# The second MLP product by Strassen's seven block products, in blocks of 256 positions

## The chip, the cores and the metric

The kernel runs on one core of one Trainium2 chip. The metric is device time in microseconds (us). The engines are PE (TensorE: matmuls, and PEld, its weight loads), DVE (VectorE), ACT (ScalarE), POOL (GpSimd) and SP (SyncE, which issues most DMAs here).

## The reference

A block of a network on 2048 positions (S) with 512 features (D): a spectral filter by a two-dimensional Fourier transform, then an MLP with 1376 hidden features (F), each with layer normalization, modulated shift and scale, and a gate. All numbers are float32.

```python
mod = (_silu(c) @ w_mod).reshape(c.shape[0], 6, 1, -1)
sa, ca, ga, sb, cb, gb = (mod[:, 0], mod[:, 1], mod[:, 2], mod[:, 3], mod[:, 4], mod[:, 5])
h = _layernorm(x, axis=-1) * (1 + ca) + sa
x = x + ga * irfft2(rfft2(h) * (A_w_r + 1j * A_w_i))
h = _layernorm(x, axis=-1) * (1 + cb) + sb
u = h @ B_w1 + B_b1
x = x + gb * ((u * tanh(softplus(u))) @ B_w2)
```

## The kernel before

Three stages compute the spectral part, all on tiles of 128 positions. The first (`p1_*`) transforms rows and columns, the second (`p2_*`) multiplies by the filter, the third (`p3_col`, `p3_row`) transforms back and adds the result to `x`, which stays on the chip as 16 tiles of 128 positions by 512 features. The MLP follows.

Matmuls of the MLP take their operands as pairs of two F32R numbers, a high part and a low part (the rest of the subtraction), and a product is three matmuls: high by high, high by low, low by high. So each operand has to be split: ACT or DVE copies the high part, DVE or POOL subtracts it for the low part. The weights `w1` (`w1h`, `w1l`), the gated weights `w2`, the normalized input `h2` and the activations (`ah`, `al`) are all split like this.

The MLP before works on 4 blocks of 512 positions and, within a block, on 11 feature tiles (10 of 128 features and one of 96). `up(g)` makes one feature tile for 512 positions: 12 matmuls (three terms by four input tiles of 128). `mish(g)` applies Mish on ACT and splits the result. `down(g)` adds the tile's product with `w2` to four PSUM banks, one for each 128 positions: 12 matmuls of 512 columns. `down` runs two steps behind `up` (`LAG = 2`). After the last feature tile DVE adds the four banks to `x` and SP stores them. The normalized input of the next block is made meanwhile by `norm_pair` (ACT), `transpose_in` (PE) and `split_in` (ACT and DVE).

The order on each engine is written out by hand: under `tc.manual_schedule()` every engine runs its instructions in program order. Tiles of the pool `work` with one tag share two buffers (`buf(tag)`); a new tile waits until all users of the one before the last are done. The loop over `s` from 0 to 16 interleaves the third stage with the preparation of the MLP: at step `s` PE does `p3_col(s)`, whose result ACT copies to `e`, and then `p3_row(s - 1)`, which reads the copy; then DVE adds it to `x`. In the same loop SP loads `w1` in 12 pieces (`load_w1`, buffers of the tags `y` and `g2` in turn), ACT and POOL split them (`split_w1`), and from step 12 on `w2` is loaded, multiplied by the gate `gbr` on POOL (`load_w2`) and split by ACT and DVE (`split_w2`). `norm_sums` and `norm_scale` make the statistics for the second normalization. The loop after it runs `mlp(s)`.

Of the kernel before, what the change touches and what calls it, by code (L numbers as in the profile page):

```python
# [7 lines left out]
F32 = mybir.dt.float32  # L8
F32R = mybir.dt.float32r
# [10 lines left out]
LAG = 2  # L20
LEAD = 8
OUT = ("BBCC", "DDBB", "CCDD")
SPARE = "DCB"
# [3 lines left out]
def tile_spectral_block(ctx: ExitStack, tc: tile.TileContext, x_d, w1_d, b1_d, w2_d,  # L27
# [542 lines left out]
    act = ctx.enter_context(tc.tile_pool(name="act", bufs=LAG + 1))  # L570
    w1h = pm.tile([P, 4, F], F32R, name="w1h")
    w1l = pm.tile([P, 4, F], F32R, name="w1l")
    w1v = w1_d.rearrange("(k p) f -> p k f", p=P)
# [19 lines left out]
    def h2_tiles(b):  # L593
        if b % 2 == 0:
            h2[b] = [pm.tile([P, 4, 512], F32R, name=f"h2{i}", tag=f"h2{i}") for i in range(2)]
        else:
            h2[b] = [big.tile([P, 4, 512], F32R, name=f"h2{i}", tag=t) for i, t in enumerate(("cr", "ci"))]
# [4 lines left out]
    def transpose_in(n, tag):  # L602
        b, j = divmod(n, 4)
        if j == 0:
            h2_tiles(b)
        pts = [bank(tag), bank(tag)]
        for i, h in enumerate(st.pop(("h2", n))):
            for k in range(4):
                nc.tensor.transpose(pts[k // 2][:, (2 * (k % 2) + i) * P:(2 * (k % 2) + i + 1) * P],  # L609
                                    h[:, k * P:(k + 1) * P], ident)  # L610
        st["pt2", n] = pts

    def split_in(n):
        b, j = divmod(n, 4)
        pts = st.pop(("pt2", n))
        for g in range(2):
            t = buf("t")
            for e in range(2):
                k = 2 * g + e
                nc.scalar.activation(t[:, 256 * e:256 * e + 256], pts[g][:, 256 * e:256 * e + 256],  # L620
                                     AF.Identity, bias=cols[:, 1, 0, k:k + 1], scale=cols[:, 1, 1, k:k + 1])
            tv = t.rearrange("p (k s) -> p k s", k=2)
            hh, hl = (v[:, 2 * g:2 * g + 2, j * P:j * P + 256] for v in h2[b])
            nc.vector.tensor_copy(hh, tv)
            nc.vector.tensor_tensor(hl, tv, plain(hh), op=ALU.subtract)
# [22 lines left out]
    w2 = {}  # L648

    def load_w2(f):  # L650
        if f in (0, 6):
            w2[f // 6] = big.tile([P, 6, 2, D], F32R, name="w2", tag=("da", "db")[f // 6])
        rows = min(P, F - f * P)
        r = buf("y")[:rows]
        nc.sync.dma_start(r, w2_d[f * P:f * P + rows, :])
        nc.gpsimd.tensor_tensor(r, r, gbr[:rows], op=ALU.mult)  # L656
        st["w2", f] = r

    def split_w2(f):
        r = st.pop(("w2", f))  # L660
        w = w2[f // 6][:r.shape[0], f % 6]
        nc.scalar.copy(w[:, 0, :], r)
        nc.vector.tensor_tensor(w[:, 1, :], r, plain(w[:, 0, :]), op=ALU.subtract)
# [6 lines left out]
    ups, acts, out_ps = {}, {}, {}  # L670

    def up(g):
        b, f = divmod(g, NF)
        rows = min(P, F - f * P)
        ps = bank("C" if g < 2 else "A")[:rows]
        fs = slice(f * P, f * P + rows)
        hh, hl = h2[b]
        parts = [(w, h, k) for w, h in ((w1h, hh), (w1l, hh), (w1h, hl)) for k in range(4)]
        for i, (w, h, k) in enumerate(parts):
            nc.tensor.matmul(ps, w[:, k, fs], h[:, k, :], start=(i == 0), stop=(i == 11))  # L680
        ups[g] = rows, ps

    def mish(g):
        rows, ps = ups.pop(g)
        w = act.tile([P, 512], F32, name="mw", bufs=2)[:rows]
        ah = act.tile([P, 512], F32R, name="ah")[:rows]
        al = act.tile([P, 512], F32R, name="al")[:rows]
        nc.scalar.activation(w, ps, AF.Mish, bias=b1n[:rows, g % NF:g % NF + 1])  # L688
        nc.vector.tensor_copy(ah, w)  # L689
        nc.vector.tensor_tensor(al, w, plain(ah), op=ALU.subtract)  # L690
        acts[g] = ah, al

    def down(g):
        b, f = divmod(g, NF)
        ah, al = acts.pop(g)
        rows = ah.shape[0]
        if f == 0:
            out_ps[b] = [bank(t) for t in OUT[b % 3]]
        for j in range(4):
            for i, (a, w) in enumerate(((ah, 0), (ah, 1), (al, 0))):  # L700
                nc.tensor.matmul(out_ps[b][j], a[:, j * P:(j + 1) * P], w2[f // 6][:rows, f % 6, w, :],  # L701
                                 start=(f == 0 and i == 0), stop=(f == NF - 1 and i == 2))
        if f == NF - 1:
            for j in range(4):
                n = 4 * b + j
                nc.vector.tensor_tensor(x[:, n, :], x[:, n, :], out_ps[b][j], op=ALU.add)
                nc.sync.dma_start(ov[:, n:n + 1, :], x[:, n:n + 1, :])

    total = 4 * NF
    ctx.enter_context(tc.manual_schedule())  # L710

    def mlp(s):
        b, f = divmod(s, NF)
        nxt = 4 * (b + 1)
        if b < 3 and f in (3, 6):
            norm_pair(nxt + 2 * (f // 6))
        if b < 3 and f in (4, 7):
            transpose_in(nxt + 2 * (f // 7), SPARE[b])
        if 2 <= s < total:
            up(s)  # L720
            mish(s)
        if s >= LAG:
            down(s - LAG)
        if 2 <= s < 9:
            split_w2(s + 2)
        if 2 <= s < 8:
            load_w2(s + 3)
        if b < 3 and f in (4, 7):
            split_in(nxt + 2 * (f // 7))

    apply_gate()
    for s in range(N2 + 1):
        if s < N2:
            p3_col(s)
        if s < 12:
            load_w1(s)
        else:
            load_w2(s - 12)
        if s >= 1:
            p3_row(s - 1)  # L740
        if s in (7, 9):
            transpose_in(s - 7, "D")
        if 2 <= s < 14:
            split_w1(s - 2)
        if s >= 13:
            split_w2(s - 13)
# [12 lines left out]
    for g in range(2):  # L759
        mish(g)  # L760
    for s in range(2, total + LAG):
        mlp(s)

# [135 lines left out]
```

## Time and profile before

| | us |
|---|---|
| median of 3 runs (412.29 to 415.01) | 413.64 |
| the profiled execution's own time | 413.82 |
| its span, from the first to the last instruction | 411.7 |
| PE busy in the span | 398.1 (97%) |
| DVE, ACT, POOL busy | 193.8, 150.6, 88.3 |
| first `p3_col` to last `p3_row` | 110.1 to 158.0 |
| last matmul of the MLP starts | 407.4 |

The mean granted clock of TensorE was 0.996 of full speed. Of the pairs of numbers in a group's row, the first is its busy time in us and the second the mean duration of one instruction in ns; matmuls are pipelined, so the distance from one matmul's start to the next is shorter than its duration. In rows of the timeline the first number is the start in us and the second the time to the end of the last of the `x` instructions.

### The profile page before, as it was taken

The numbers are of one execution on the slowest core, as the hardware profiler recorded it, in microseconds if no ns is written. First come the engines' busy times: TensorE is split into PE (matmuls) and PEld (weight loads), VectorE is DVE, ScalarE is ACT, GpSimd is POOL, SyncE is SP. The second block draws the span as 40 slices with busy tenths as digits, with TensorE's granted clock in tenths as the row PEclk, the third lists the DMA queues.
The fourth block names the chain that finished last, engine by engine and source line by source line (L and its number), as shares of the span: only waits on it lengthen the run. The fifth ranks groups of instructions, "written<-read, shape, count | busy, mean of one in ns | idle before, by whom it ended". The sixth has DMA issues, their size and how long they took to land.

```text
span 411.7 us, 5922 instructions
## 1 busy us (share of the span) xinstructions
PE 398.1 (97%) x2273; PEld 342.9 (83%) x2273; DVE 193.8 (47%) x374; ACT 150.6 (37%) x326; POOL 88.3 (21%) x116
## 2 busy tenths in 40 slices
PE   8999889999999998899999999999999999999996
PEld 8888778899899997688878888878888878888874
DVE  2999949676256886444521342411432312422212
ACT  2777754576746734423411222311232310111110
POOL 0677625576122445212100000000000000000000
PEclk9999999999999999899999999999999999999999
DMA  8999961381313232011000200000200000200002
GB/s 288 340 332 375 280 252 53 102 311 50 94 34 81 68 78 77 27 52 34 13 0 2 102 0 2 0 0 2 102 2 0 0 2 0 102 2 0 0 2 102
DMA packets 20603, 34.58 MB, mean 84 GB/s; under 512 B 3680, under 2 KB 6528, under 8 KB 20192
## 3 DMA queue, kind: packets, MB, share of 16 engines
q1 hardware_dynamic: 20144, 33.68, 24.7%
q10 hardware_dynamic: 432, 0.53, 0.4%
q8 instruction: 18, 0.29, 0.3%
q14 instruction: 9, 0.07, 0.1%
HBM read 30.01 MB, written 4.19 MB: 83 GB/s over the span
## 4 chain that ended last, share of the span: by engine, by line
PE 85%; DVE 9%; ACT 2%; issue 2%; POOL 1%; POOLq 0%; ACTq 0%
PE bank L680 30%; PE bank L701 29%; PE bank L633 4%; PE bank L643 4%; PE bank L634 3%; PE bank L452 3%; PE bank L498 3%; DVE ve L121 2%; DVE st L108 2%; PE bank L609 2%; PE bank L485 2%; PE bank L431 1%; DVE buf L223 1%; DVE buf L203 1%; PE bank L269 1%
## 5 line engine op out<-in xcount | busy, mean ns | idle before, releaser
L701 PE MATMUL bank<-w,ah 128*128 128x512 f32 (+1 forms) x352 | 109.9, 394 | 2.5 <-issue 2.5
L688 ACT ACTIVATE mw<-bank,b1n 128x512 f32<-128x512 f32 (+1 forms) x44 | 30.1, 687 | 183.0 <-PE bank L680 129.2
L680 PE MATMUL bank<-h,w1h 128*128 128x512 f32 (+1 forms) x352 | 96.8, 397 | 0.0
L689 DVE CAST ah<-mw 128x512 fp32r<-128x512 f32 (+1 forms) x44 | 20.3, 461 | 159.1 <-ACT mw L688 159.1
L701 PEld LDWEIGHTS bank<-w,ah 128*128 128x128 f32 (+1 forms) x352 | 66.9, 190 | 17.3 <-issue 2.9
L680 PEld LDWEIGHTS bank<-h,w1h 128*128 128x128 f32 (+1 forms) x352 | 65.0, 187 | 15.1
L701 PE MATMUL bank<-w,al 128*128 128x512 f32 (+1 forms) x176 | 69.0, 392 | 0.0
L680 PE MATMUL bank<-h,w1l 128*128 128x512 f32 (+1 forms) x176 | 48.1, 396 | 0.0
L680 PEld LDWEIGHTS bank<-h,w1l 128*128 128x128 f32 (+1 forms) x176 | 32.9, 187 | 8.1
L701 PEld LDWEIGHTS bank<-w,al 128*128 128x128 f32 (+1 forms) x176 | 33.4, 190 | 7.3 <-DVE al L690 0.2
L690 DVE TENSOR_TENSOR al<-mw,ah 128x512 fp32r<-128x512 f32 (+1 forms) x44 | 30.4, 692 | 4.2
L230 PE MATMUL bank<-buf,mring 128*128 128x512 f32 x48 | 21.4, 446 | 4.3 <-DVE buf L223 1.9
L633 PE MATMUL bank<-kc,d 128*128 128x128 f32 x128 | 24.9, 276 | 0.5 <-ACT d L356 0.5
L634 PE MATMUL bank<-kc,d 128*128 128x128 f32 x128 | 24.8, 275 | 0.0
L108 DVE BATCH_NORM_STATS2 st<-x 128x6 f32<-128x512 f32 x32 | 22.0, 688 | 3.8 <-DMA x<-in_A_x_dram 3.4
L656 POOL TENSOR_TENSOR buf<-buf,modr 128x512 f32<-128x512 f32 (+1 forms) x11 | 14.6, 1327 | 35.7 <-DMA buf<-in_B_w_dram 35.7
L589 POOL TENSOR_TENSOR w1l<-buf,w1h 128x512 fp32r<-128x512 f32 (+1 forms) x12 | 14.5, 1215 | 27.1 <-ACT w1h L588 27.1
L633 PEld LDWEIGHTS bank<-kc,d 128*128 128x128 f32 x128 | 19.4, 192 | 0.7 <-ACT d L356 0.7
L634 PEld LDWEIGHTS bank<-kc,d 128*128 128x128 f32 x128 | 19.4, 192 | 0.0
L643 PE MATMUL bank<-kiv,buf 128*128 128x128 f32 x128 | 17.1, 276 | 0.0
L646 DVE TENSOR_TENSOR x<-x,bank 128x512 f32<-128x512 f32 x16 | 10.8, 675 | 13.0 <-PE bank L643 13.0
L188 PE MATMUL bank<-modr,xring 128*128 128x128 f32 x128 | 16.9, 276 | 0.0
(134 smaller groups left out, 555.2 us busy)
## 6 DMA issues: line engine op xcount, KB each, us to landing
buf<-in_B_w_dram SPq DMA_DIRECT2D x18, 256.0 KB, 2.6
xring<-in_x_t_dram SPq DMA_DIRECT2D x16, 256.0 KB, 4.7
x<-in_A_x_dram SPq DMA_DIRECT2D x16, 256.0 KB, 5.3
wm<-in_w_mod_dram SPq DMA_DIRECT2D x16, 256.0 KB, 4.3
out_dram<-x SPq DMA_DIRECT2D x16, 256.0 KB, 2.1
mraw<-in_km_dram SPq DMA_DIRECT2D x16, 128.0 KB, 4.8
wqa<-in_w_q_dram SPq DMA_DIRECT2D x8, 256.0 KB, 4.0
wqb<-in_w_q_dram SPq DMA_DIRECT2D x8, 256.0 KB, 4.8
```

Of the source, the lines that this page charges most:

```text
L108: nc.vector.bn_stats(t, x[:, n, :])
L188: nc.tensor.matmul(pgv[:, j], data(j), krs[:, j, :].rearrange("p (c q) -> p c q", c=2), start=True, stop=True)
L230: nc.tensor.matmul(pa, m[:, a, 0:128], g, start=(i == 0), stop=False)
L633: nc.tensor.matmul(o, dj[:, 0:128], kc[0][:, n, :], start=True, stop=False)
L634: nc.tensor.matmul(o, dj[:, 64:192], kc[1][:, n, :], start=False, stop=True)
L643: nc.tensor.matmul(px[:, j * P:(j + 1) * P], e[:, j * P:(j + 1) * P], kiv[:, j, :], start=True, stop=True)
L656: nc.gpsimd.tensor_tensor(r, r, gbr[:rows], op=ALU.mult)
L680: nc.tensor.matmul(ps, w[:, k, fs], h[:, k, :], start=(i == 0), stop=(i == 11))
L688: nc.scalar.activation(w, ps, AF.Mish, bias=b1n[:rows, g % NF:g % NF + 1])
L689: nc.vector.tensor_copy(ah, w)
L690: nc.vector.tensor_tensor(al, w, plain(ah), op=ALU.subtract)
L701: nc.tensor.matmul(out_ps[b][j], a[:, j * P:(j + 1) * P], w2[f // 6][:rows, f % 6, w, :], start=(f == 0 and i == 0), stop=(f == NF - 1 and ...
```

## The change

The second product is made by Strassen's algorithm on pairs. Two feature tiles (the rows of a 2 by 2 block matrix), two groups of 128 positions and two halves of the 512 output features make a product of 2 by 2 blocks. Seven products of sums and differences of the blocks take the place of eight. This is the variant with few additions: four sums on the side of the activations and four on the side of `w2`, and a few on the outputs.

- The MLP works on 8 blocks of 256 positions (`NB`). Within a block there are 6 steps (`NT`): step 0 takes the feature tile of 96 alone and in the plain way, steps 1 to 5 take a pair of feature tiles each.
- `up` makes both tiles of a pair, side by side in one bank: 24 matmuls of 256 columns.
- `mish` applies Mish in two halves, makes four sums of 128 by 128 on DVE into `u`, and copies the high parts on ACT (before, DVE did). `low` subtracts the low parts, after `down(s - 1)` in the program.
- `down` makes seven products, each of three matmuls of 256 columns, into six banks. It runs one step behind `up`.
- At the end of a block ACT copies four of the banks (`gather`), POOL sums them (`chain`) and adds them to `x` (`spread`), DVE adds the two others (`residual`), and SP stores two tiles. After the last block DVE takes a part of POOL's work.
- `w2` is prepared pair by pair: `load_w2` loads the two tiles, `sum_w2` multiplies both by the gate and makes four differences of 256 columns into the one buffer `tsum`, all on POOL, and `split_w2` copies and subtracts 256, 512 and 1024 columns (ACT and DVE). The table `prep` says at which step of the third stage this is done; pairs 4 and 5 are prepared in the MLP's first steps.
- `w1`'s pieces now use the buffers of the tag `g2` alone, and `w2`'s those of `y`.
- Of the next block's input, the first two tiles alone are prepared in the third stage, and `transpose_in` and `split_in` work in halves.

```diff
-LAG = 2
+NT = 6
+NB = 8
+TERMS = ((0, 0), (0, 1), (1, 0))
+RAW = ((0, None, 0, 0), (1, 0, 2, 1), (2, 0, 1, 6))
+SUM = ((3, None, 3, 3), (4, None, 4, 4), (5, None, 5, 5), (1, 1, 6, 2))
+LAST = (RAW[0], *SUM[0:3], RAW[1], RAW[2], SUM[3])
...
     def load_w1(i):
         k, lo, hi = piece(i)
-        r = buf(("y", "g2")[i % 2])[:, 0:hi - lo]
+        r = buf("g2")[:, 0:hi - lo]
...
+    def load_w2(t):
+        st["w2", t] = rs = []
+        for e, f, rows in tiles(t):
+            r = buf("y")[:rows]
+            nc.sync.dma_start(r, w2_d[f * P:f * P + rows, :])
+            rs.append(r)
+
+    def sum_w2(t):
+        rs = st["w2", t]
+        for r in rs:
+            nc.gpsimd.tensor_tensor(r, r, gbr[:r.shape[0]], op=ALU.mult)
+        if t:
+            u, v = rs
+            for o, a, b in ((0, u[:, 256:], u[:, 0:256]), (1, v[:, 256:], tsum[:, 0]),
+                            (2, v[:, 256:], u[:, 256:]), (3, v[:, 0:256], tsum[:, 1])):
+                nc.gpsimd.tensor_tensor(tsum[:, o], a, b, op=ALU.subtract)
+
+    def split_w2(t):
...
+            cut = ((rs[0][:, 0:256], 0, 256), (rs[1], 256, 768), (tsum.rearrange("p e d -> p (e d)"), 768, 1792))
+            parts = [(r, flat[0][:, a:b], flat[1][:, a:b]) for r, a, b in cut]
+        for r, h, l in parts:
+            nc.scalar.copy(h, r)
+            nc.vector.tensor_tensor(l, r, plain(h), op=ALU.subtract)
...
+    def up(g):
+        b, t = divmod(g, NT)
+        ups[g] = ps = bank("A")
+        hh, hl = h2[b]
+        parts = [(w, h, k) for w, h in ((w1h, hh), (w1l, hh), (w1h, hl)) for k in range(4)]
+        for e, f, rows in tiles(t):
+            for i, (w, h, k) in enumerate(parts):
+                nc.tensor.matmul(ps[:rows, 256 * e:256 * e + 256], w[:, k, f * P:f * P + rows], h[:, k, :],
+                                 start=(i == 0), stop=(i == 11))
...
+    def mish(g):
+        b, t = divmod(g, NT)
+        ps = ups.pop(g)
+        w = buf("g1")
+        for e, f, rows in reversed(tiles(t)):
+            c = slice(256 * e, 256 * e + 256)
+            nc.scalar.activation(w[:rows, c], ps[:rows, c], AF.Mish, bias=b1n[:rows, f:f + 1])
+        hi, lo = (act.tile([P, 7, P], F32R, name=n) for n in ("ah", "al"))
...
+            for o, p, q, op in ((v[:, 0], a[:, 0], a[:, 2], ALU.add), (v[:, 1], v[:, 0], a[:, 1], ALU.subtract),
+                                (v[:, 2], a[:, 1], a[:, 0], ALU.subtract), (v[:, 3], a[:, 3], v[:, 1], ALU.subtract)):
+                nc.vector.tensor_tensor(o, p, q, op=op)
+            parts = [(w[:, P:], slice(0, 3)), (u, slice(3, 7))]
...
+            nc.scalar.copy(h, r)
+            flat.append((l, r, plain(h)))
+        return flat
+
+    def low(parts):
+        for l, r, h in parts:
+            nc.vector.tensor_tensor(l, r, h, op=ALU.subtract)
...
+        for n, half, e, r in LAST if g == NB * NT - 1 else RAW + SUM:
+            o = out[n][:, 0:256] if half is None else out[n][:, 256 * half:256 * half + 256]
+            for i, (p, q) in enumerate(TERMS):
+                nc.tensor.matmul(o, a[p][:, e], w2[t][q][:, r], start=(half is None and t == 1 and i == 0),
+                                 stop=(t == 5 and i == 2 and (n, half) != (1, 0)))
+
+    def gather(b):
+        out = out_ps[b]
+        p, q = buf("h"), buf("h")
+        for o, k in ((p[:, 0:256], 0), (q[:, 0:256], 4), (q[:, 256:], 5), (p[:, 256:], 3)):
+            nc.scalar.copy(o, out[k][:, 0:256])
+        done[b] = p, q
+
+    def chain(b, eng):
+        p, q = done[b]
+        eng.tensor_tensor(q[:, 0:256], q[:, 0:256], p[:, 0:256], op=ALU.add)
+        eng.tensor_tensor(q[:, 256:], q[:, 256:], q[:, 0:256], op=ALU.add)
+
+    def residual(b):
+        for n, ps in ((2 * b + 1, out_ps[b][1]), (2 * b, out_ps[b][2])):
+            nc.vector.tensor_tensor(x[:, n, :], x[:, n, :], ps, op=ALU.add)
+
+    def spread(b, ea, eb):
+        p, q = done.pop(b)
+        u, v = x[:, 2 * b + 1, :], x[:, 2 * b, :]
+        ea.tensor_tensor(u, u, p, op=ALU.add)
+        ea.tensor_tensor(v[:, 256:], v[:, 256:], p[:, 256:], op=ALU.add)
+        eb.tensor_tensor(u[:, 256:], u[:, 256:], q[:, 0:256], op=ALU.add)
+        vv = v.rearrange("p (j d) -> p j d", j=2)
+        eb.tensor_tensor(vv, vv, q[:, 256:].unsqueeze(1).to_broadcast([P, 2, 256]), op=ALU.add)
...
     def mlp(s):
+        b, t = divmod(s, NT)
+        nxt = 2 * b + 2 if b < NB - 1 else None
+        if s < total:
             up(s)
+        if t in (3, 4) and nxt:
+            transpose_in(nxt, t - 3)
+        parts = mish(s) if s < total else ()
+        if t == 2 and nxt:
+            norm_pair(nxt)
+        down(s - 1)
+        if t == 0:
+            gather(b - 1)
+            if s == total:
+                chain(b - 1, nc.vector)
+            residual(b - 1)
+        low(parts)
+        if t in (3, 4) and nxt:
+            split_in(nxt, t - 3)
+        if t == 0:
+            if s < total:
+                chain(b - 1, nc.gpsimd)
+            spread(b - 1, nc.gpsimd, nc.vector if s == total else nc.gpsimd)
+            store(b - 1)
...
+    prep = {1: (load_w2, 1), 2: (sum_w2, 1), 3: (split_w2, 1), 4: (load_w2, 2), 5: (sum_w2, 2), 8: (split_w2, 2),
+            9: (load_w2, 3), 10: (sum_w2, 3), 11: (split_w2, 3), 12: (load_w2, 0), 13: (sum_w2, 0), 16: (split_w2, 0)}
     for s in range(N2 + 1):
         if s < N2:
             p3_col(s)
         if s < 12:
             load_w1(s)
-        else:
-            load_w2(s - 12)
         if s >= 1:
             p3_row(s - 1)
-        if s in (7, 9):
-            transpose_in(s - 7, "D")
+        if s in (7, 8):
+            transpose_in(0, s - 7)
         if 2 <= s < 14:
             split_w1(s - 2)
+        if s in prep:
+            prep[s][0](prep[s][1])
         if s >= 1:
             norm_sums(s - 1)
...
-        if s in (4, 6):
-            norm_pair(s - 4)
-        if s in (7, 9):
-            split_in(s - 7)
-        if s >= 15:
-            up(s - 15)
+        if s == 4:
+            norm_pair(0)
+        if s in (7, 8):
+            split_in(0, s - 7)
+        if s == 16:
+            up(0)
+    low(mish(0))
+    load_w2(4)
+    sum_w2(4)
+    for s in range(1, total + 1):
         mlp(s)
+        if s == 2:
+            split_w2(4)
+            load_w2(5)
+            sum_w2(5)
+        if s == 4:
+            split_w2(5)
```

More of the change, by code (lines that the diff above doesn't have):

```diff
@@ L613, in split_in, with transpose_in @@
[L613 to L625, printed above, removed]
+    def transpose_in(n, g):
+        if g == 0:
+            h2_tiles(n // 2)
+        st["pt2", g] = ps = bank("A" if n else "D")
+        hs = st["h2", n]
+        for k in range(2):
+            for i, h in enumerate(hs):
+                nc.tensor.transpose(ps[:, (2 * k + i) * P:(2 * k + i + 1) * P],
+                                    h[:, (2 * g + k) * P:(2 * g + k + 1) * P], ident)
@@ new lines, in tiles @@
+    def tiles(t):
+        return [(0, NF - 1, F - (NF - 1) * P)] if t == 0 else [(e, 2 * t - 2 + e, P) for e in range(2)]
+    def load_w2(t):
[13 more added lines that the diff above has]
+                nc.gpsimd.tensor_tensor(tsum[:, o], a, b, op=ALU.subtract)
@@ L683, in mish @@
     def mish(g):
[L684 to L691, printed above, removed]
-    def down(g):
[L694 to L707, printed above, removed]
@@ L710, in tile_spectral_block @@
+    total = NB * NT
     ctx.enter_context(tc.manual_schedule())
     def mlp(s):
[L713 to L719, printed above, removed]
-            up(s)
[L721 to L727, printed above, removed]
```

111 lines of the change are left out of this document (65 added, 46 removed).

## The prediction, made before the changed kernel was run

> **What bounds the kernel now.** I read the page first, then the chain of work in order of time, then a table by stages, and last single instructions where the change lands.
>
> ```profile
> PE 398.1 (97%) x2273; PEld 342.9 (83%) x2273; DVE 193.8 (47%) x374; ACT 150.6 (37%) x326; POOL 88.3 (21%) x116
> ...
> PE 85%; DVE 9%; ACT 2%; issue 2%; POOL 1%; POOLq 0%; ACTq 0%
> ```
>
> PE carries 85% of the chain that ended last. The table by stages (us; busy time and count of PE, PEld, DVE, ACT, POOL; clock) tells where PE is without a gap:
>
> ```profile
> 113.90:126.50 12.60, 12.60 (x116) 12.60 (x115) 8.05 (x21) 6.06 (x14) 3.47 (x3) 1.00 0.22 57
> 126.50:140.00 13.50, 13.50 (x122) 13.41 (x121) 8.42 (x20) 8.62 (x20) 4.84 (x4) 1.00 0.26 68
> 140.00:154.30 14.30, 14.30 (x129) 14.30 (x128) 12.58 (x25) 7.47 (x17) 7.34 (x6) 1.00 0.27 73
> 154.30:166.10 11.80, 9.29 (x46) 7.38 (x44) 7.42 (x17) 5.40 (x9) 6.87 (x6) 1.00 0.26 68
> 166.10:405.80 239.70, 239.70 (x1060) 195.60 (x1061) 73.20 (x131) 51.86 (x85) 6.47 (x5) 0.99 0.06 19
> ```
>
> So the third stage (`p3_col`, `p3_row`, 110 to 158) and the MLP are both bound by PE alone. In the third stage DVE is busy for 62 to 88%, ACT for 48 to 64% and POOL for 28 to 51%. The chain of work, at the start of the MLP, in its steady part and at the end (start us, us):
>
> ```profile
> 157.11 0.89 PE bank L643 x8
> 158.00 5.59 PE bank L680 x24
> 163.59 2.50 issue
> 166.08 4.57 PE bank L701 x12
> ...
> 205.51 2.80 PE bank L680 x12
> 208.31 2.72 PE bank L701 x12
> ...
> 405.77 0.69 DVE x L706
> 406.46 2.05 DVE x L706 x3
> ```
>
> One `up` of 12 matmuls takes 2.80 us (233 ns each, 512 columns), one `down` 2.72 (227 ns). 44 of each are 243 us.
>
> **What the MLP's matmuls cost afterwards.** All of `up` and the Strassen part of `down` become 256 columns wide. The trace has such matmuls, at L231 and L232, among 512-wide ones:
>
> ```profile
> 27.45 0.28 PE L231 MATMUL bank<-buf,mring 128*128 128x256 f32 x1
> 27.57 0.28 PE L232 MATMUL bank<-buf,mring 128*128 128x256 f32 x1
> 27.69 0.40 PE L230 MATMUL bank<-buf,mring 128*128 128x512 f32 x1
> 27.92 0.28 PE L231 MATMUL bank<-buf,mring 128*128 128x256 f32 x1
> ```
>
> Two of 256 and one of 512 take 0.47 us from start to start, so 117.5 ns per 256 columns. From below it is bounded by the 128-wide matmuls, 111 ns each (0.89 us for 8 at L643), where the weight load and not the stream must set the pace; from above by the 3% between L680 and L701 for one shape: 121. I take 117.5, the only row of this shape.
>
> `down`: per pair of feature tiles and 256 positions, 7 products x 3 terms = 21 matmuls x 117.5 = 2.47 us, where 12 x 227 = 2.72 stood. 40 such steps save 10.2 us; the eleventh feature tile (6 matmuls of 512 columns per block) costs the same. The multiplications fall by an eighth, the time by 9%, since a narrower matmul carries its own weight load. `up`: 24 x 117.5 = 2.82 against 2.80, 44 times: +0.9. The transposes number 64 either way. Net -9.3.
>
> The Trainium skill, "TensorE: Matmul & The Clock Gate" (LDWEIGHTS; Back-to-back issue gap), speaks against narrowing: a load of 128 weight columns takes 128/1.2 = 107 ns whatever the stream, as long as 256 columns take. Its table has 262 cycles for 256 columns, 109 ns; by that the sum would be lower by 1896 x 8 ns = 15 us, an estimate from the page. The trace does not follow it: it gives 216 ns for 512 columns and the rows say 227 to 233.
>
> **Does PE stay fed in the MLP?** The lag between `up` and `down` falls from 2 to 1. After `up(s)` come two Mish, four adds of 128 columns, two copies and two subtractions:
>
> ```profile
> L688 ACT ACTIVATE mw<-bank,b1n 128x512 f32<-128x512 f32 x40 | 27.4, 687 | 163.7 <-PE bank L680 109.9 <-issue 52.5 <-DVE al L690 1.3
> L690 DVE TENSOR_TENSOR al<-mw,ah 128x512 fp32r<-128x512 f32 x40 | 27.7, 692 | 3.7
> L636 ACT COPY buf<-bank 128x512 f32<-128x512 f32 x16 | 9.3, 580 | 8.4 <-PE bank L634 8.4
> L356 ACT COPY d<-bank 128x256 f32<-128x256 f32 x30 | 11.3, 377 | 3.0 <-PE bank L498 3.0
> ```
>
> Estimated by width from these: 0.9 + 1.2 + 0.6 + 0.7, with hops 3.8 us; `down(s)` starts 2.47 + 2.82 = 5.3 us after `up(s)` ends. That is hidden. At a block's end `gather`, `residual` and POOL's 6 us of `chain` and `spread` lie under the next block's first steps; the `h` buffers are wanted again 10 us later. At the last block nothing covers the chain: `down` can start after 2.47, and waits about 0.8 for `low`. In the tail the last store then waits for a DVE add (0.7), two POOL adds (1.33 + 0.85, rows below) and another DVE add (0.7) in a row, 3.7 with the hops, where one DVE add of 0.68 followed the last matmul: +3.0.
>
> **The preparation of w2** is what I expect to decide. Before, 11 multiplications on POOL. Now `sum_w2(t)` is two multiplications and four 256-wide subtractions, and `split_w2(t)` copies and subtracts 1792 columns. Rows for POOL, ACT, DVE, and the load:
>
> ```profile
> L656 POOL TENSOR_TENSOR buf<-buf,modr 128x512 f32<-128x512 f32 x10 | 13.3, 1331 | 31.4 <-DMA buf<-in_B_w_dram 31.4
> L474 POOL TENSOR_TENSOR buf<-buf 128x256 f32<-128x256 f32 x15 | 13.5, 902 | 4.5 <-DVE buf L468 2.7 <-PE bank L485 1.7
> L181 POOL TENSOR_TENSOR mring<-mraw,mring 128x256 fp32r<-128x256 f32 x16 | 13.0, 815 | 16.6 <-ACT mring L180 16.6
> L589 POOL TENSOR_TENSOR w1l<-buf,w1h 128x512 fp32r<-128x512 f32 x8 | 10.3, 1289 | 20.9 <-ACT w1h L588 20.9
> L588 ACT CAST w1h<-buf 128x512 fp32r<-128x512 f32 x8 | 5.0, 626 | 0.0
> L137 ACT ACTIVATE buf<-x,nmr,rstd 128x512 f32<-128x512 f32 x16 | 12.1, 804 | 2.9 <-issue 2.9
> L108 DVE BATCH_NORM_STATS2 st<-x 128x6 f32<-128x512 f32 x32 | 22.0, 688 | 3.8 <-DMA x<-in_A_x_dram 3.4
> buf<-in_B_w_dram SPq DMA_DIRECT2D x18, 256.0 KB, 2.6
> ```
>
> One `sum_w2` is 2 x 1.33 + 4 x 0.85 = 6.1 us of POOL (0.85 between the 815 and 902 rows). Three fall into the third stage, whose step is 2.68 us. Their total fits; the order does not. Queues run in program order, and PE's `p3_row(n)` waits for ACT's copy `e(n)`, which now stands behind copies that wait for POOL. Walked on the old clock:
>
> ```profile
> 116.69 0.58 ACT L636 COPY buf<-bank 128x512 f32<-128x512 f32 x1 [2.11 <-PE bank L634]
> 117.17 0.62 ACT L588 CAST w1h<-buf 128x512 fp32r<-128x512 f32 x1
> ...
> 117.87 1.27 POOL L589 TENSOR_TENSOR w1l<-buf,w1h 128x512 fp32r<-128x512 f32 x1 [11.70 <-ACT w1h L588]
> ...
> 124.48 1.06 PE L643 MATMUL bank<-kiv,buf 128*128 128x128 f32 x8
> ...
> 124.56 0.29 ACT L113 ACTIVATE rstd<-mv,eps 128x2 f32<-128x2 f32 x1 [1.59 <-DVE mv L109]
> 124.89 0.20 ACT L114 ACTIVATE rstd<-rstd 128x2 f32<-128x2 f32 x1
> ...
> 162.94 1.28 ACT L688 ACT_TABLE_LOAD   x1
> ```
>
> 1. POOL ends `w1l(0)` at 119.1, `sum_w2(1)` at 125.2. ACT's copy of `tsum` (1024 columns: 1.1, an estimate from 0.38 at 256 and 0.63 at 512) ends at 126.3, `e(4)` behind it at 126.9. `p3_row(4)` was due at 124.5: 2.5 late.
> 2. DVE's subtraction for `tsum` (1.2) ends at 127.6; behind it statistics, add, statistics (2.5), then ACT's Ln and Exp (0.55), two norms (1.5), `e(5)`: 132.8. PE had work until 129.6: 3.2.
> 3. `sum_w2(2)` follows `w1l(3)` at 134.7 and ends at 140.8, `w1l(4)` at 142.1. w1 now has two buffers, not four, so piece 6 can only then be fetched: 144.8. ACT stands at its copy since 139, then copies w2 (2.1), waits for DVE (2.2) and does Ln, Exp and `split_in` before `e(9)` at 151.9. PE ran dry at 144.4: 7.5.
> 4. The rows for `sum_w2(3)` stand in SP's queue behind w1's piece 9, which waits for `w1l(7)` at 153.8. They land at 156.7, the sums end at 162.7, `e(12)` at 164.4; PE dry at 160.0: 4.4.
> 5. As in 2, `e(13)` at 168.8, PE dry at 167.1: 1.7.
>
> Together 19.3. Instructions follow one another a little closer than their durations (116.69 to 117.17 with 0.58 busy), so I take 18, within 12 and 20 (12 if the first and third wait are each halved). A stall of 2.5 us has a second price in this trace, the clock (last but two column):
>
> ```profile
> 167.00:168.00 1.00, 1.00 (x4) 0.78 (x4) 0.97 (x3) 1.00 (x3) 0.00 (x0) 0.50 0.07 16
> ```
>
> After the stall at 163.59 the clock was 0.50, and the 12 matmuls at 166.08 took 4.57 instead of 2.72. Such losses fall into the next wait for ACT here and add nothing. In exchange that old stall (2.50, and 1.85 of slow clock) shrinks: after the last `p3_row`, PE has `up(0)` and `up(1)`, 4.2 us, against some 6 for DVE's add and statistics, the table load (1.3) and the first Mish. About 1.8 is left: -2.6.
>
> **Sum.** -10.2 + 0.9 + 18 - 2.6 + 0.8 + 3.0 = +9.9 us. The profiled execution took 413.8 (span 411.7 and 2.1 around it), 0.2 above the runs' median of 413.6. Forecast 423.7.
>
> **Rivals.**
> - *The preparation stays hidden; faster.* Without the waits of the third stage: 423.7 - 18 = 405.7. For it: POOL is busy for only a third of that stage. Against: ACT's order. It is decided at the first `tsum`: if POOL ended at 122, 3 us sooner than in my walk, `e(4)` would be in time, and so on down the list. That needs 256-wide sums at a quarter of their rows' durations. 16%.
> - *The pace of 256 columns is the weight load's,* 111.5 ns as in the 128-wide rows: 1896 x 6 ns = 11 us less, 412.5: no change. For it: both are one load and one stream per matmul; against: the four rows at 27.45. 10%. The page named above goes further, to 109 ns; the same four rows speak against it.
> - *121 ns,* if operands lie as badly as for L680 at 512: 1896 x 3.5 = 6.6 more, 430.3. 8%.
> - My forecast: 66%.
>
> **From these to the numbers.** About 1% (4.1 us) is what a measurement of this kernel can tell from no change. Faster by more: the first rival, 0.16. Within: the second and a sliver of the forecast with its waits at 12, 0.13. Slower: 0.71. The range goes from 411 (between the first two rivals) to 431 (the third).
>
> **What would show it.** Right: PE idle in the third stage before the matmuls of `p3_row`, released by ACT's copy `e`, in four or five places of 2 to 8 us; ACT idle on POOL's `tsum`; the MLP starting 15 to 18 us later; a step of `up` and `down` of 2.82 + 2.47 without gaps; clock 0.5 after the waits. Wrong: no PE gap before the first `up`, or a 256-wide pace below 114 or above 121 ns; or gaps inside the MLP from `low` or from POOL's `spread`, which I priced at nothing.

## The result, and the profile after

The changed kernel took 427.62 us (median of 4 runs, 426.98 to 429.38) against 413.86 for the kernel before on the same chip: ratio 1.034, 95% interval 1.030 to 1.039. It is slower by 3.4%. The profiled execution took 427.3 us with a span of 425.3; the matching one of before had 413.8 and 411.7, so there are 13.5 us to account for.

The page of the changed kernel first (busy us, share of the span, instructions; then the shares of the chain that ended last):

```profile
PE 396.7 (93%) x3161; PEld 384.1 (90%) x3161; DVE 259.7 (61%) x543; ACT 220.3 (52%) x495; POOL 145.8 (34%) x180
...
PE 64%; DVE 17%; ACT 6%; issue 5%; POOL 5%; DMA 2%; DVEq 0%; POOLq 0%; ACTq 0%
```

PE's busy time hardly moved (398.1 before); its share of the chain fell from 85% to 64%. What came in is DVE, ACT and POOL, all of them busier: work that used to lie beside PE is now in front of it. The table by stages says where (us; busy time and count of PE, PEld, DVE, ACT, POOL; granted clock; DMA):

```profile
110.87:126.50 15.63, 14.56 (x128) 14.37 (x128) 7.84 (x13) 5.79 (x14) 7.76 (x8) 1.00 0.05 13
126.50:140.00 13.50, 9.83 (x73) 9.64 (x74) 8.69 (x20) 7.28 (x15) 8.03 (x9) 0.87 0.30 92
140.00:158.00 18.00, 13.32 (x97) 13.12 (x96) 11.80 (x22) 7.63 (x16) 8.11 (x8) 0.81 0.32 97
158.00:172.84 14.84, 11.74 (x102) 11.33 (x101) 9.83 (x21) 5.68 (x12) 10.09 (x10) 1.00 0.15 45
172.84:182.85 10.01, 8.78 (x66) 8.07 (x66) 7.38 (x17) 4.53 (x9) 4.37 (x5) 1.00 0.08 28
182.85:418.30 235.45, 234.77 (x1935) 232.62 (x1934) 129.38 (x292) 119.38 (x250) 46.06 (x48) 1.00 0.05 19
```

Nearly all holes are in the third stage, between 122 and 173 us. The fifth row adds 1.2 us at the MLP's start, and the last row, the rest of the MLP, has PE busy for 234.77 of 235.45 us. The waits of the whole span (us in total, times, the longest) name the releaser, and the timeline shows the first of the five places:

```profile
PE bank L647 <- ACT buf L640: 12.5, 5, 4.7
...
ACT w L696 <- POOL modr L684: 2.9, 1, 2.9
```

```profile
124.77 1.17 POOL L684 TENSOR_TENSOR modr<-buf,modr 128x256 f32<-128x256 f32 x1
...
125.98 1.05 ACT L696 CAST w<-modr 128x1024 fp32r<-128x1024 f32 x1 [2.94 <-POOL modr L684]
126.93 0.58 ACT L640 COPY buf<-bank 128x512 f32<-128x512 f32 x1
...
127.56 1.16 PE L647 MATMUL bank<-kiv,buf 128*128 128x128 f32 x8 [2.13 <-ACT buf L640]
```

Read it from below: PE's `p3_row(4)` (L647) waits for ACT's copy `e(4)` (L640); ACT stood for 2.94 us at the copy of `tsum` (L696), which is ahead of `e(4)` in its queue; and that waited for POOL's fourth subtraction (L684). The rows before `p3_row` 4, 5, 9, 12 and 13 start 2.40, 2.89, 4.96, 2.17 and 1.48 us after the matmul ahead of them, 0.11 of which is the usual distance: 13.35 us of waiting. Behind the second and the third PE runs slowly (the same columns as above, clock 0.58 and 0.60):

```profile
133.10:136.60 3.50, 3.48 (x18) 3.48 (x19) 1.71 (x4) 1.48 (x3) 2.94 (x3) 0.58 0.17 42
...
151.00:157.90 6.90, 6.85 (x38) 6.85 (x39) 4.01 (x8) 2.65 (x6) 3.71 (x4) 0.60 0.46 152
```

That loses 3.5 x 0.42 + 6.9 x 0.40 = 4.2 us of PE's work.

The chain in the MLP's steady part and at the end:

```profile
207.13 2.84 PE bank L714 x24
209.97 1.38 PE bank L755 x6
211.35 2.84 PE bank L714 x24
214.19 2.52 PE bank L761 x21
...
416.43 0.76 PE bank L761 x4
...
418.65 0.70 DVE x L778
...
419.48 1.27 POOL x L783
...
420.78 0.93 DVE x L785
```

`up` of a pair (L714) takes 2.84 us; a Strassen step of `down` (L761) is 21 matmuls 120 ns apart, 2.52 us; the single tile (L755) takes 1.38. After the last matmul DVE, POOL and DVE again stand in one row, as forecast.

### The profile page after: what moved, and what is told of

Same layout as the page of the kernel before. It is cut to its first block, busy times and chain, and to the rows that moved or that the text cites. A ratio compares the mean times of both kernels' runs of the same rounds, so it can differ in the third digit from the quotient of the medians.

```text
span 425.3 us, 8110 instructions
## 1 busy us (share of the span) xinstructions
PE 396.7 (93%) x3161; PEld 384.1 (90%) x3161; DVE 259.7 (61%) x543; ACT 220.3 (52%) x495; POOL 145.8 (34%) x180
## 4 chain that ended last, share of the span: by engine, by line
PE 64%; DVE 17%; ACT 6%; issue 5%; POOL 5%; DMA 2%; DVEq 0%; POOLq 0%; ACTq 0%
PE bank L714 26%; PE bank L761 20%; PE bank L455 3%; PE bank L755 3%; PE bank L501 3%; DVE st L111 3%; DMA buf<-in_B_w_dram 2%; POOL modr L684 2%; DVE ve L124 2%; POOL buf L679 2%; PE bank L488 2%; DVE buf L734 1%; PE bank L434 1%; DVE buf L226 1%; DVE buf L206 1%
## 5 line engine op out<-in xcount | busy, mean ns | idle before, releaser
L734 DVE TENSOR_TENSOR buf<-buf 128x128 f32<-128x128 f32 x160 | 52.2, 367 | 70.9 <-ACT buf L723 69.4
L723 ACT ACTIVATE buf<-bank,b1n 128x256 f32<-128x256 f32 (+1 forms) x88 | 37.3, 470 | 74.4 <-PE bank L714 74.4
L740 ACT CAST ah<-buf 128x512 fp32r<-128x512 f32 (+2 forms) x88 | 48.6, 552 | 38.7 <-DVE buf L734 37.1
L746 DVE TENSOR_TENSOR al<-buf,ah 128x512 fp32r<-128x512 f32 (+2 forms) x88 | 54.9, 624 | 10.0 <-ACT ah L740 10.0
L714 PE MATMUL bank<-h2o,w1h 128*128 128x256 f32 (+1 forms) x352 | 52.8, 282 | 0.0
L714 PE MATMUL bank<-h,w1h 128*128 128x256 f32 (+1 forms) x352 | 52.7, 282 | 0.0
L714 PEld LDWEIGHTS bank<-h2o,w1h 128*128 128x128 f32 (+1 forms) x352 | 46.5, 186 | 0.3
L714 PEld LDWEIGHTS bank<-h,w1h 128*128 128x128 f32 (+1 forms) x352 | 46.4, 186 | 0.3
L761 PE MATMUL bank<-w2a,ah 128*128 128x256 f32 x168 | 36.8, 286 | 0.0
L761 PE MATMUL bank<-w2b,ah 128*128 128x256 f32 x168 | 36.3, 283 | 0.0
L647 PE MATMUL bank<-kiv,buf 128*128 128x128 f32 x128 | 19.3, 300 | 12.5 <-ACT buf L640 12.5
L647 PEld LDWEIGHTS bank<-kiv,buf 128*128 128x128 f32 x128 | 17.4, 211 | 13.5 <-ACT buf L640 13.5
L761 PEld LDWEIGHTS bank<-w2b,ah 128*128 128x128 f32 x168 | 28.2, 191 | 0.0
L761 PEld LDWEIGHTS bank<-w2a,ah 128*128 128x128 f32 x168 | 28.1, 191 | 0.0
L714 PE MATMUL bank<-h,w1l 128*128 128x256 f32 (+1 forms) x176 | 28.0, 282 | 0.0
L714 PE MATMUL bank<-h2o,w1l 128*128 128x256 f32 (+1 forms) x176 | 28.0, 282 | 0.0
```

The costliest lines, as they stand in the source:

```text
L647: nc.tensor.matmul(px[:, j * P:(j + 1) * P], e[:, j * P:(j + 1) * P], kiv[:, j, :], start=True, stop=True)
L714: nc.tensor.matmul(ps[:rows, 256 * e:256 * e + 256], w[:, k, f * P:f * P + rows], h[:, k, :], start=(i == 0), stop=(i == 11))
L723: nc.scalar.activation(w[:rows, c], ps[:rows, c], AF.Mish, bias=b1n[:rows, f:f + 1])
L734: nc.vector.tensor_tensor(o, p, q, op=op)
L740: nc.scalar.copy(h, r)
L746: nc.vector.tensor_tensor(l, r, h, op=ALU.subtract)
```

## Experiments

Ratios are to the kernel before on the same chip and in the same series. Later line numbers shift by a few, because lines were added.

**1. POOL's subtractions left out.** In `sum_w2`:

```diff
-        if t:
+        if False:
             u, v = rs
             ...
                 nc.gpsimd.tensor_tensor(tsum[:, o], a, b, op=ALU.subtract)
```

> The changed kernel without POOL's four subtractions per `sum_w2`: the two multiplications and all copies stay, so `tsum` holds old numbers and the product with the summed columns of w2 is left out of the computation. Theory (PE waits in the third stage because ACT's copy `e` stands in its queue behind the copy of `tsum`, which waits for POOL): POOL has 3.4 us less to do per pair, the waits before rows 4, 5, 9, 12 and 13 (13.4 us, and some 4 us of half clock behind them) shrink by about half: about 419 us, MLP 8 us earlier, its steps as before. Rival (ACT and DVE themselves are too full with the added copies and subtractions, POOL is only named): within 2 us of 427.

Measured: 420.2 us, ratio 1.016 (1.012 to 1.020), 7.4 us less than the changed kernel.

```profile
PE bank L647 <- ACT buf L640: 8.6, 4, 4.0
```

```profile
131.93 1.38 PEld L647 LDWEIGHTS bank<-kiv,buf 128*128 128x128 f32 x8 [4.16 <-ACT buf L640]
```

(First the waits, then the timeline at row 5.) That is the theory's size. But the wait before row 4 is gone and the one before row 5 has grown from 2.6 to 4.0: there ACT waits 4.76 us for DVE's statistics, which stand behind DVE's 1.95 us subtraction for `tsum`. So POOL's four subtractions are about half of the cause. Of the four waits that are left, those before rows 5, 9 and 13 stand behind DVE's subtractions for w2, and the one before row 12 behind POOL's two multiplications, which this run kept.

**2. w1 in four buffers.**

```diff
-        r = buf("g2")[:, 0:hi - lo]
+        r = buf(("t", "g2")[i % 2])[:, 0:hi - lo]
```

> The changed kernel with w1's pieces in four buffers (tags `t` and `g2` in turn) instead of two. Theory: only the wait before row 9 has w1's late piece 6 in it (a gap of 4.9 us and two windows of half clock behind it); it shrinks, and the one before row 12 a little: about 424 us, first two gaps unchanged at 2.4 and 2.9 us. Rival (the wait before row 9 is POOL's sums alone): within 1 us of 427.4.

Measured: 423.4 us, ratio 1.024 (1.020 to 1.027). The step before row 9 fell from 4.96 to 3.54 us, those before rows 4 and 5 stayed (2.40, 2.88), that before row 12 fell from 2.17 to 0.62. w1's late piece had a part in it; the change of tags cost 4.4 us (0.0107 of 413.5) by itself.

**3. The kernel before in narrow matmuls.** All eight products, the same order, each 512-wide matmul of `up` and of `down` (but for each block's first tile) as two of 256:

```diff
-        for i, (w, h, k) in enumerate(parts):
-            nc.tensor.matmul(ps, w[:, k, fs], h[:, k, :], ...)
+        for c in (slice(0, 256), slice(256, 512)):
+            for i, (w, h, k) in enumerate(parts):
+                nc.tensor.matmul(ps[:, c], w[:, k, fs], h[:, k, c], ...)
```

> The kernel before, all eight products, same order; only `up` and `down` (all feature tiles but the first of each block) are cut into matmuls of 256 columns, two for each of 512. Theory (a 256-wide matmul costs 120 ns here, so that Strassen's seventh lost is largely given back): up 24 x 118.5 = 2.84 instead of 2.80, down 24 x 120 = 2.88 instead of 2.72: 44 x 0.04 + 40 x 0.16 = +8 us, about 422. Rival (120 ns is caused by what is special in the Strassen order, its banks and operands, and plain halves cost 113 to 116): 410 to 416.

Measured: 421.1 us, ratio 1.018 (1.014 to 1.022), 7.8 us above the kernel before in its series. The chain, `down` and `up` in turn:

```profile
209.19 2.88 PE bank L703 x24
212.06 2.84 PE bank L681 x24
```

24 matmuls of 256 take 2.88 us where 12 of 512 took 2.72: 120 ns each, without any of Strassen's banks or operands. So the width costs it. This splits the gain of `down`: seven products for eight, at one width, give 2.88 - 2.52 = 0.36 us a step or 14.4 us; the narrow matmuls that the algorithm needs take 6.4 of it back there and 1.8 in `up`.

**4. The same work in another order.** POOL's sums are spread, one multiplication or two subtractions a step, and the copies come steps later. w1 has four buffers as in run 2, some loads of w2 come later, and pair 3's split moves out of the third stage into the MLP's first steps:

```diff
-    prep = {1: (load_w2, 1), 2: (sum_w2, 1), 3: (split_w2, 1), 4: (load_w2, 2), 5: (sum_w2, 2), 8: (split_w2, 2), ...
+    prep = {2: [(lo, 1)], 3: [(su, 1, (0,))], 4: [(su, 1, (1,))], 5: [(su, 1, (2, 3)), (sp, 1, (0, 1))],
+            6: [(su, 1, (4, 5)), (lo, 2)], 8: [(su, 2, (0,))], 9: [(sp, 1, (2,)), (su, 2, (1,))], ...
```

> The changed kernel with the preparation of w2 in another order, nothing left out: POOL's sums spread one multiplication or two subtractions to a step, each copy of `tsum` placed steps behind its sums, w1 in four buffers, the first pair's rows in the tag `h`, pair 3's split put off to the MLP's second step. Theory (order, not amount, makes the 13.4 us of waits and the 4 us of slow clock): third stage without waits over 1 us, MLP about 15 us earlier, 412 to 414 us, about as before. Rival (the amount of work on POOL and ACT is too large to hide): 420 or more, with waits in other places.

Measured: 415.6 us, ratio 1.006 (1.004 to 1.009): by the two ratios 11.5 us less than the changed kernel, with nothing left out, and 415.6 where 412 to 414 were expected. The five waits are now two (first the waits, then ACT's timeline at the MLP's start):

```profile
PE bank L647 <- ACT buf L640: 1.3, 2, 1.0
```

```profile
160.21 0.30 ACT L116 ACTIVATE rstd<-mv,eps 128x4 f32<-128x4 f32 x1 [4.09 <-DVE mv L112]
160.54 0.21 ACT L117 ACTIVATE rstd<-rstd 128x4 f32<-128x4 f32 x1
160.76 1.28 ACT L724 ACT_TABLE_LOAD   x1
```

So it was not the amount of work that made the waits, for nothing is left out. How the 11.5 us divide is open in part: the four buffers were worth 4.4 by themselves in run 2, and what pair 3's later split gives was not measured alone; the rest is the order. The last three rows show what holds the MLP's start: ACT idles 4.09 us for DVE's last statistics, and Mish's table and the first Mish stand behind two short instructions that only the last two blocks (tiles 12 to 15) need.

**5 and 6. Is the slow clock a price of its own?** Idle matmuls fill the waits of the changed kernel:

```diff
         px = bank("B")
+        for _ in range({5: 22, 9: 40, 12: 24, 13: 8}.get(n, 0)):    # sixth run: {5: 12, 9: 18, 12: 20, 13: 6}
+            nc.tensor.matmul(px[:, 0:P], kc[0][:, 0, :], kiv[:, 0, :], start=True, stop=True)
```

> The changed kernel with idle matmuls of 128 columns put into the waits of the third stage (22 before row 5, 40 before row 9, 24 before row 12, 8 before row 13, 112 ns each; the rows overwrite their result), so that TensorE's clock isn't lowered behind them. Theory (clock loss falls into the next wait and adds nothing): the half-clock stretches (3.4 and 6.8 us) go, the waits before rows 12 and 13 grow by as much as PE is faster (before row 12 from 2.1 to some 4.8 us), the time stays at 427 within 1.5 us. Rival (the slow clock has a price of its own): 423 to 424.

Measured: 432.7 us, ratio 1.046 (1.042 to 1.050), which neither expected. Each of these matmuls is two instructions:

```profile
146.09 9.10 PE L647 MATMUL bank<-kiv,kc 128*128 128x128 f32 x80
149.65 0.58 ACT L640 COPY buf<-bank 128x512 f32<-128x512 f32 x1
...
155.03 1.06 PE L649 MATMUL bank<-kiv,buf 128*128 128x128 f32 x8
```

`e(9)` was there at 150.2, the fillers ran to 155.0: they were the delay. With counts that fit:

> As the run with idle matmuls in the third stage's waits, with fewer of them: each is two instructions of 112 ns, so 12, 18, 20 and 6 (2.7, 4.0, 4.5 and 1.3 us) before rows 5, 9, 12 and 13 are what the waits hold; the first counts were twice too long. Theory (clock loss falls into the next wait): no half clock, ACT's `e(12)` and `e(13)` no earlier than in the changed kernel, since POOL's sums set them, and 427 within 1.5 us. Rival (the slow clock has a price of its own): `e(12)` about 2.5 us earlier and 423 to 424.

Measured: 428.1 us, ratio 1.033 (1.030 to 1.036), as the changed kernel (1.034). First the changed kernel, then this run (whose third stage begins 0.45 us later): the copies `e(11)` and `e(12)` in the timeline, and the row of the table by stages over the stretch from the one wait to the other:

```profile
156.63 0.58 ACT L640 COPY buf<-bank 128x512 f32<-128x512 f32 x1 [4.25 <-PE bank L638]
...
163.22 0.58 ACT L640 COPY buf<-bank 128x512 f32<-128x512 f32 x1
```

```profile
150.85:163.75 12.90, 10.91 (x72) 10.72 (x72) 6.53 (x12) 5.07 (x11) 9.20 (x9) 0.78 0.25 83
```

```profile
154.75 0.59 ACT L640 COPY buf<-bank 128x512 f32<-128x512 f32 x1 [1.70 <-PE bank L638]
...
164.26 0.58 ACT L640 COPY buf<-bank 128x512 f32<-128x512 f32 x1
```

```profile
151.30:164.20 12.90, 12.49 (x111) 12.49 (x112) 6.76 (x11) 4.87 (x9) 8.95 (x9) 1.00 0.25 83
```

With full clock PE reaches `e(11)` 2.3 us sooner, and `e(12)` comes no sooner: POOL sets it. The theory holds; at half clock PE only did slowly what it would have waited for.

**7. Statistics out of the way.** In the kernel of run 4:

```diff
-        if s in (8, 12, 16):
-            norm_scale(s - 4, s)
+        if s in (10, 14):
+            norm_scale(s - 6, s - 2)
...
+        if s == 17:                      # in the MLP
+            norm_scale(12, 16)
```

> The kernel with the sums spread, and besides ACT's Ln and Exp for the second normalization taken out of PE's way: those for tiles 4 to 7 and 8 to 11 two steps later, those for 12 to 15 in the MLP's third block. Theory (the first Mish waits, behind these two instructions, for DVE's last statistics, and the stall lowers the clock): the stall before the first `down` (1.9 us) and the half clock behind it (1.7 us) go, and the waits before rows 7 and 11 (1.1 and 0.5 us) too: about 5 us less, 410 to 411. Rival (weights of w2 or the Mish's table load itself hold the first `down`): within 1.5 us of 415.6.

Measured: 418.4 us, ratio 1.010 (1.006 to 1.013), 1.4 us above run 4 by the ratios. The theory's number is missed; the rival's is met by the ratios, but not for its reason. The stall before the first `down` did go, and new ones came (from one start to the next): 2.8 and 1.8 us in the third stage, 2.7 and 1.3 at 177 and 183, 1.4 at 265. In the third stage DVE's small instructions (L124) and a subtraction now met POOL's sums: one of 128 by 1024 took 3.64 us, 1.22 in run 4.

**8. And the end changed.** Three products of the last block's pair 4 are held back into pair 5's, the sums go into `x` before `residual`:

```diff
+            todo = [(a, t, HEAD[0]), *r[0:2], *((a, t, p) for p in HEAD[1:]), r[2], *((a, t, p) for p in REST)]
...
+                finish(b - 1)
```

> As the kernel with the sums spread and the late statistics, and the end changed: three products of pair 4 in the last block are held back into pair 5's (they cover the wait for `low`, 0.4 us), the banks that feed the output sums are finished 1.4 us ahead of the last matmul, and these sums go into `x` before `residual`; also the first block's `norm_pair` one step earlier. Theory: 1.5 to 2 us less than the kernel it is made from, about 409. Rival (POOL and DVE slow each other at the end as in the MLP's first steps): no gain over that kernel.

Measured: 419.1 us, ratio 1.012 (1.009 to 1.015), not distinguishable from run 7. From the last matmul's start to the end it is 6.1 us instead of 6.9, but the wait for `low` grew by 0.26, and the earlier `norm_pair` made the stall at 180 us 4.0 instead of 2.7.

**9. The statistics in the kernel before.** There the last four alone moved:

```diff
-        if s in (8, 12, 16):
+        if s in (8, 12):
             norm_scale(s - 4, s)
...
+        if s == 20:                      # in the MLP
+            norm_scale(12, 16)
```

> The kernel before, with the last four tiles' Ln and Exp moved from the end of the third stage into the MLP's second block, nothing else. Theory (its stall of 2.5 us at 163.6 and the 1.85 us of slow clock behind it hang on these two instructions, not on Mish): about 4.3 us less, 409.3. Rival (the first Mish and its split set the first `down` anyway): within 1 us of 413.5.

Measured: 410.7 us, ratio 0.991 (0.989 to 0.993), the fastest kernel of the study and 3.7 us under before in its series: the theory, 0.6 short of its size. The timeline, and the clock behind the start:

```profile
162.16 1.28 ACT L688 ACT_TABLE_LOAD   x1
...
164.70 0.70 PE L701 MATMUL bank<-w,ah 128*128 128x512 f32 x2 [0.74 <-PE bank L680]
```

```profile
164.70:169.00 4.30, 4.30 (x18) 3.25 (x19) 4.23 (x6) 2.63 (x5) 1.82 (x1) 1.00 0.10 35
```

The first `down` starts 1.4 us sooner and the clock behind it is 1.00, not 0.50. What is left of the stall hangs on w2's copies ahead of the table load.

**10. Start and end on run 4's third stage.** Only the last four statistics moved (behind the MLP's step 13), with the end of run 8.

> The kernel with the sums spread, its third stage left as it was but for the Ln and Exp of tiles 12 to 15, which go into the MLP's third block (second step), and with the changed end. Theory: the stall and slow clock at the MLP's start (3.6 us) go and the end gives 0.6: 4 us less than with the sums spread alone, ratio to the kernel before 0.995 to 1.000. Rival (the earlier start meets POOL's sums for pairs 4 and 5, which slow DVE's adds, and the wait only moves to the MLP's third step): ratio 1.002 to 1.008, with gaps of over 2 us before `up` at 175 to 185.

Measured: 418.1 us, ratio 1.009 (1.006 to 1.012): the rival, just above its range. The first `down` is 2 us sooner and at full clock, and three waits (from one start to the next) take it back, 2.8 us before `up` at 176, 2.8 and 3.0 before transposes at 182 and 241. ACT's row at the first:

```profile
174.18 1.04 ACT L697 CAST w2b<-modr 128x1024 fp32r<-128x1024 f32 x1 [2.78 <-POOL modr L685]
175.13 0.83 ACT L724 ACTIVATE buf<-bank,b1n 128x256 f32<-128x256 f32 x2
```

Mish stands behind the copy of `tsum`, which waits for POOL: the trap of the third stage once more, where I had priced a gap in the MLP at nothing. The second wait is another: behind DVE's four adds of 128 columns, which took 3.61 us beside POOL's sums.

**11. That trap taken away.** The copy of `tsum` for pairs 4 and 5 one step later, with pair 4's the sums of pair 5, and the statistics behind step 15:

```diff
-            split_w2(4)
+            split_w2(4, (0, 1))
             load_w2(5)
-            sum_w2(5)
+        if s == 3:
+            split_w2(4, (2,))
+            sum_w2(5)
...
-        if s == 13:
+        if s == 15:
             norm_scale(12, 16)
```

> As the kernel with the sums spread, the early start and the changed end, with two moves: in the MLP's first block the copy of `tsum` for pairs 4 and 5 is queued on ACT one step later than its sums on POOL (in the run before, Mish stood 2.8 us behind a copy that waited for POOL), and the Ln and Exp of tiles 12 to 15 follow the step with t = 3 instead of t = 1 (there, with three table loads, they made a gap of 2.9 us at 240). Theory (the two gaps are ACT's order again): both shrink by 2 us or more each, ratio to the kernel before 0.996 to 1.001, so the Strassen version at most equals the kernel before, and doesn't reach the kernel before with late statistics (0.991). Rival (DVE's adds, slowed beside POOL to 3.6 us, set these steps): ratio 1.004 or more, with a gap of over 2 us left at 175 to 185.

Measured: 412.7 us, ratio 0.997 (0.994 to 0.999): the theory. The gaps at 176 and 182 are gone, 3.4 us are left in four pieces between 183 and 191, and 0.3 near 244. Pair 5's sums moved too, so this run does not tell which of the moves closed the gap at 182. This is the best Strassen version. It is 0.3% below before, but run 9, with its one edit, is further below (0.989 to 0.993, in another series); so nothing here shows Strassen ahead of eight products in an order as good.

**12. DVE beside POOL.** Three multiplications a step on POOL, results unused, in the kernel before:

```diff
+        if 22 <= s < 38:
+            for i in range(3):
+                nc.gpsimd.tensor_tensor(buf("y"), gbr, gbr, op=ALU.mult)
```

> The kernel before with three multiplications of 128x512 on POOL added to each of the MLP's steps 22 to 37, results unused (about 4 us of 5.5). It compares DVE's instructions of one line with and without POOL beside them. Theory (an instruction of DVE with two operands in SBUF cannot run beside POOL's reads): the subtraction for `al` (two SBUF operands, 0.69 alone) takes 1 to 2 us in these steps; the copy `ah` about doubles too (0.43 alone), an add to `x` with one operand in PSUM stays at 0.69; the time as before, since the lag of two steps hides it. Rival (POOL slows DVE only through small pieces or through what they share in data): all stay as alone.

Measured: 413.0 us, a single run, within the range of the kernel before (412.7 to 415.3). POOL ran them in one stretch from 205 to 257 us. DVE's groups there, and then from 257 to 405:

```profile
L690 DVE TENSOR_TENSOR al<-mw,ah 128x512 fp32r<-128x512 f32 x9 | 12.1, 1349 | 0.9
L689 DVE CAST ah<-mw 128x512 fp32r<-128x512 f32 x9 | 8.5, 942 | 15.9 <-ACT mw L688 15.9
...
L706 DVE TENSOR_TENSOR x<-x,bank 128x512 f32<-128x512 f32 x4 | 2.5, 674 | 0.0
```

```profile
L690 DVE TENSOR_TENSOR al<-mw,ah 128x512 fp32r<-128x512 f32 x23 | 15.9, 692 | 2.3
L689 DVE CAST ah<-mw 128x512 fp32r<-128x512 f32 x23 | 9.8, 427 | 89.4 <-ACT mw L688 89.4
L706 DVE TENSOR_TENSOR x<-x,bank 128x512 f32<-128x512 f32 x8 | 4.9, 679 | 0.0
```

The subtraction of two SBUF tiles goes from 692 to 1349 ns and the copy from 427 to 942, as the theory has it; the add that reads one operand from PSUM stays.

## Why the prediction was right, and where it was off

The direction, the place and the mechanism held; the forecast was 3.9 us short of the median (423.7 against 427.6).

| term | forecast, us | measured, us | from |
|---|---|---|---|
| `down` | -10.2 | -7.8 | 40 x (2.52 - 2.72), and 8 x (1.38 - 1.36) for the single tile |
| `up` | +0.9 | +1.8 | 44 x (2.84 - 2.80) |
| five waits | +18 | +17.5 | 13.35 of waiting, about 4.2 of half clock |
| MLP's start | -2.6 | -3.1 | gap of 1.2 for 2.5 and 1.85 of slow clock |
| last `low` | +0.8 | +0.4 | 0.50 instead of 0.12 from start to start, before the second product's low part |
| tail | +3.0 | +2.6 | 6.9 for 4.3 from the last matmul's start to the end |
| not forecast | 0 | +0.6 | a wait for `low` at 204, behind w2's split on DVE |
| not forecast | 0 | +0.8 | stages before: `p3_col` begins at 110.87, not 110.08 |

That makes +12.8 of 13.5. Of the other 0.7, 0.4 is the first single tile of `down` at 178 us, which takes 1.82 us instead of 1.38; the rest I could not name.

**The step that failed is the price of a narrow matmul.** From "two of 256 and one of 512 take 0.47 us" the prediction took a quarter, 117.5 ns per 256 columns. That counts the wide one as two narrow ones. The wide one's own price stood beside it, 227 ns: (470 - 227) / 2 = 121.5. The same rows also show it without a sum: the starts at 27.45, 27.57 and 27.69 lie 0.12 us apart, and run 3 measured 120 ns. At the measured pace (120 ns in `down`, 118 in `up`) the two terms come out 3.3 us dearer. On the profiled execution the miss is 3.6 us; that the other terms hardly show in it is luck: waits, start, `low` and tail were forecast 1.8 us too dear, and 2.1 us were not forecast at all. So the rival of 121 ns was closest to the truth, and at 8% too small; the weight load's 111.5 ns does not set this pace. The Trainium skill, "TensorE: Matmul & The Clock Gate" (Back-to-back issue gap), has 109 ns for this width, as the gap of an isolated matmul. The trace does not agree for this stream, in which every matmul loads its weights: 120.

**The waits** came at the five rows named. The rival "the preparation stays hidden" was to be decided by the end of the first `tsum`: 125.9 here, in a third stage that begins 0.8 later, against 125.2 in the walk; 122 would have been needed. Single waits came out otherwise than walked: those before rows 9 and 12 were 4.9 and 2.1 us instead of 7.5 and 4.4, but half clock behind the wait ahead of each had already cost PE 1.5 and 2.8 us, which is the rule "falls into the next wait" at work. Run 6 bears that rule out, run 4 that order and buffers and not the amount make the waits, run 1 that POOL's subtractions are half of it, run 2 that w1's two buffers have a share in the third wait and the fourth.

**Priced at nothing, and not nothing:** gaps inside the MLP. The prediction named `low` and POOL's `spread` as their makers. In the changed kernel, with its late start, there is the wait of 0.6 us for `low`; run 10, whose MLP starts 16 us earlier, showed 5.6 us at 176 and 182, and they came from POOL's sums for w2, not from `spread`.

## What to carry over

An algorithm that saves multiplications by smaller blocks pays for each block's width: price the narrow instruction against the wide one of the same row before counting the saved ones (here 14.4 us saved, 8.2 given back). Where engines run in program order, a copy that waits for a slow helper must not stand ahead of a copy that the busiest engine waits for; the same work in another order, with two more buffers for w1, was worth 11.5 us. And look at the old kernel with the new knowledge: its best gain here was a few short instructions moved (two of ACT and four of DVE), not the new algorithm.

## What the runs showed of the hardware

**POOL beside it slows DVE, by kind of operand.** Run 12 shows it by itself: 692 to 1349 ns, 427 to 942, and 679 to 674. In the changed kernel DVE's four 128-wide adds take 1.02 us, 2.91 beside POOL:

```profile
179.06 2.91 DVE L734 TENSOR_TENSOR buf<-buf 128x128 f32<-128x128 f32 x4
...
183.93 1.02 DVE L734 TENSOR_TENSOR buf<-buf 128x128 f32<-128x128 f32 x4 [0.58 <-ACT buf L723]
```

The Trainium skill, "SBUF — State Buffer" (Who interferes with whom), says that a DVE instruction with two SBUF inputs and a POOL instruction that reads SBUF cannot run together, since DVE's second input uses POOL's port, and that one with a single SBUF input is free unless it is in a two-port mode. The subtraction and the add with an operand in PSUM agree. The copy has a single SBUF input and is slowed, which agrees if it runs in a two-port mode; its 427 ns against the subtraction's 692 for the same width fit that, but no row names the mode.

**Half clock does not follow from the length of a pause alone.** The pause of 2.3 us before row 4 left the clock at 1.00 in the changed kernel; in run 6 the same pause was followed by 0.50. One microsecond behind that pause in each, first the changed kernel, then run 6 (clock in the last column but two):

```profile
128.00:129.00 1.00, 1.00 (x11) 1.00 (x10) 0.97 (x3) 0.00 (x0) 1.00 (x1) 1.00 0.69 190
```

```profile
129.00:130.00 1.00, 1.00 (x7) 1.00 (x6) 0.96 (x3) 0.00 (x0) 0.52 (x1) 0.50 0.61 211
```

The Trainium skill, "TensorE: Matmul & The Clock Gate" (Part 1: The HAM clock gate), tells of free-running windows of 3.4 us, and has half clock after at least one idle window. The slow stretches agree with such windows: by the clock of each microsecond they last 3.4 us behind row 5 (132.6 to 136.1) and 6.8 behind row 9 (149.7 to 156.5), one and two of them. The idle time does not agree: 2.3 us in run 6 and 2.8 before row 5 were enough. That it depends on where in a window the pause falls would fit both, but no run here shows it.
